# Products of k and v in a linear-attention kernel: one matmul a head on 128x64 tiles of TensorE in place of two on 128x32

## The chip, the cores and the metric

The kernel runs on one core of a Trainium2 chip. The metric is the device time of one execution in microseconds (us). TensorE (PE in the profile) multiplies, with its weight loads listed as an engine of their own (PEld); VectorE (DVE), ScalarE (ACT) and GpSimd (POOL) do elementwise work; SyncE (SP) issues transfers.

## The reference, cut to what matters

A recurrence with decay over 768 steps, for 4 batches and 8 heads of size 48, and behind it an MLP over the 3072 tokens (384 to 2048 to 384):

```python
for t in range(S):
    kt, vt, rt = (k[:, :, t], v[:, :, t], r[:, :, t])
    cur = np.einsum('bhd,bhe->bhde', u[None] * kt, vt)
    y[:, :, t] = np.einsum('bhd,bhde->bhe', rt, state + cur)
    state = w[None, :, :, None] * state + np.einsum('bhd,bhe->bhde', kt, vt)
...
h = x @ w_in
sp = np.maximum(h, 0.0) + np.log1p(np.exp(-np.abs(h)))
return (h * erf(sp)) @ w_out
```

The recurrence is computed in chunks of 128 steps. What a chunk adds to the state is, for each head, the product of its (scaled) k, transposed, with its v: a 48x48 matrix summed over 128 steps. The change is in how this product is cut into matmuls.

## The kernel before

There are 24 chunks, numbered g: six positions in the sequence, each for four batches. A chunk's tile `att` has k and v with the 128 steps on the partitions (columns K0 on: 8 heads of 48; columns V0 on: 4 pairs of 112, the two heads of a pair at 0 and 64). The work of a chunk on TensorE is, in words of the long string `ORDER`:

- `A`: the 128x128 products of r and k (`a_step`, line 328), written as tiles of 64 rows by 64 columns, with 48 rows of data (from chunk 8 on half of them with 128 moving columns and half with 64);
- `Y`: the output y (`y_product`, line 357) on tiles of 128 rows by 32 columns, from the state `sbd` and from the masked products `am`;
- `D`: the product of k and v (`ds_product`, line 380), for the chunks 0 to 19, since the last position needs no state behind it. Per head, two matmuls with 48 moving columns of v. The output of a head of 48 rows is cut into 32 rows and the rest (32 with 16 padding rows for the first head of a pair, 16 for the second), so that four matmuls of a pair of heads lie on the four column tiles of a 128x32 array;
- `X`, `V`, `T`: small products on full or on 64-column tiles (lines 414, 266, 271, 214, 217), in the first chunks only.

All operands here are float32, and the trace shows two records of MATMUL and two of LDWEIGHTS for each matmul of line 380: 20 chunks of 16 matmuls give 640 records. The MLP runs in 96 steps, each with `f` (line 436, 9 matmuls of 128x512) and `p` (line 499, 9 matmuls of 128x512), all on full 128x128 tiles.

`ORDER` is a hand-written order of all this work: each engine executes its part in this order, and waits where an operand or a buffer isn't ready. On TensorE a `D` stands mostly between the `Y` of its chunk and the `A` of a later one, or among `f` and `p`. Its result, in a PSUM buffer, is added to the state by VectorE (`s_wide`, line 394, for the first four chunks line 396), which the `Y` of the same batch one position later reads. The PSUM buffer is one of three that the `f` steps use as well.

Of the kernel before, what the change touches and what calls it, by code (L numbers as in the profile page):

```python
# [31 lines left out]
D = 48  # L32
NPAIR = 4
PR = 112
# [5 lines left out]
V0, K0, R0, AW = 1024, 1472, 1856, 2240  # L40
# [3 lines left out]
def body(ctx: ExitStack, tc: tile.TileContext, att, attn, wucol, u, win, wout, levels, outT):  # L44
    nc = tc.nc
# [106 lines left out]
    H = C // 2  # L152
# [222 lines left out]
    def ds_product(t, home, name):  # L375
        ds = home[0].tile([PR, NPAIR, D], F32, tag=home[1], name=name)
        for h in range(8):
            hh, p = h % 2, h // 2
            for c0, c1 in ((0, 32), (32, D if hh else H)):
                nc.tensor.matmul(out=ds[64 * hh + c0:64 * hh + c1, p, :], lhsT=t[:, K0 + h * D + c0:K0 + h * D + c1],  # L380
                                 rhs=t[:, V0 + PR * p + 64 * hh:V0 + PR * p + 64 * hh + D], start=True, stop=True,
                                 skip_group_check=True)
        return ds

    def s_views(b, hh):
# [180 lines left out]
    for i, x in enumerate(words):  # L566
# [44 lines left out]
        elif what == "M":  # L611
            st_[num // 10]["am", num % 10] = diag_m(st_[num // 10]["q"], num // 10, num % 10, eng, True)
        elif what == "A":
            st_.setdefault(num, {})
            a_step(num)
        elif what == "P":
            g, hh = num // 10, num % 10
            if g in direct:
                masked(g, hh)
            else:  # L620
                whole = slice(None)
                lo, hi = slice(0, H), slice(H, None)
                parts = [(whole, whole, hi), (lo, slice(0, 1), lo), (hi, slice(1, 2), lo)]
                predicated(st_[g]["am", hh], st_[g]["ap"][hh], parts if g >= LEAN else [(whole, whole, whole)])
        elif what == "Y":
            y_step(num)
        elif what == "X":
            x_step(num, sub)
        elif what == "D":
            st_.setdefault(num, {})["ds"] = ds_product(chunks[num], (ps3, "h"), f"ds{num}")  # L630
        elif what == "S":
            s_wide(num, sub, eng)
        elif what == "F":
            fetch_w(num // 10, num % 10)
        elif what == "C":
            load_w(sub, eng, num // 10, num % 10)
        elif what == "O":
            end(sub, num // 10, num % 10)
        elif what == "W":
            keep_warm(num)  # L640
# [12 lines left out]
    with tc.If(rv > 0), tc.tile_pool(name="gen", bufs=1) as gen:  # L653
# [37 lines left out]
        with tc.For_i(0, NB, 1) as blk:  # L691
            x = xp.tile([P, 2, NQ, TB], F32R, tag="x", name="gx")
            for b in range(4):
                t = apool.tile([P, AW], F32, tag="att", name=f"gatt{b}")
# [8 lines left out]
                for l in range(7):  # L703
# [7 lines left out]
                    for hh in range(2):  # L711
                        r = slice(64 * hh, 64 * hh + D)
                        ap = psa.tile([P, NPAIR, C], F32, tag="A", name=f"gA{b}_{l}_{hh}")
                        for p in range(NPAIR):
                            nc.tensor.matmul(out=ap[:, p, :], lhsT=kl[r, p].rearrange("p n m -> p (n m)"),
                                             rhs=rl[r, p].rearrange("p n m -> p (n m)"), start=True, stop=True)
# [3 lines left out]
                nc.vector.tensor_tensor(out=t[:, K0:R0], in0=t[:, K0:R0], in1=wknf, op=ALU.mult)  # L720
                y = y_product(t, am, b, False, f"gy{b}", False, (psa, "A"))
                ds = ds_product(t, (psa, "A"), f"gds{b}")
                for hh in range(2):
                    r, sv, w128 = s_views(b, hh)
# [155 lines left out]
```

## Time and profile before

| | us |
|---|---|
| median of 3 runs | 498.16 (497.91 to 498.21) |
| the profiled execution, its own time | 497.96 |
| its span, first to last instruction | 496.2 |
| TensorE busy (matmul) in the span | 487.1 (98%) |
| TensorE weight loads | 391.9 (79%) |
| ScalarE, VectorE, GpSimd busy | 388.9, 332.9, 148.5 |
| line 380 on the chain of waits | 1% of the span |

Busy times are unions of the records of a group, so records that overlap count once; the mean beside them is that of one record from its start to its modelled end. A matmul's record is much longer than its share of the array, since matmuls follow each other in a pipeline.

### The profile page before, as it was taken

What the parts mean: (1) busy time and instruction counts of PE and PEld (TensorE: products, weight loads), DVE (VectorE), ACT (ScalarE), POOL (GpSimd) and SP (SyncE); (2) the same over time, 40 slices, a digit from 0 to 9 for tenths busy, and PEclk for the clock granted to TensorE, in tenths of its full rate; (3) what the DMA queues carried; (4) which work ended last, traced back from release to release, by engine and by line L of the source; (5) the groups of instructions that cost most, each with busy time, mean ns of one, the idle gap of its engine ahead of it and who ended that gap; (6) DMA issues with size and microseconds to landing.
All of it is one profiled execution on the core that took longest, in us unless ns stands there. A gap on an engine that the chain in (4) does not pass through costs nothing.

```text
span 496.2 us, 10958 instructions
## 1 busy us (share of the span) xinstructions
PE 487.1 (98%) x4462; PEld 391.9 (79%) x4462; DVE 332.9 (67%) x586; ACT 388.9 (78%) x700; POOL 148.5 (30%) x132
## 2 busy tenths in 40 slices
PE   7999999999999999999999999999999999999995
PEld 5777888878778888888888878887878878888884
DVE  7999866767878956746766576686664445434553
ACT  2779999998976687877568875768977788978892
POOL 8659436016321735700168062172000000000000
PEclk9999999999999999999999999999999999999999
DMA  8874653328007603100450023232010000100001
GB/s 311 328 264 179 227 214 130 126 65 305 23 1 269 195 39 113 45 1 1 128 176 0 25 92 136 94 104 85 2 42 1 22 0 1 43 22 1 0 1 69
DMA packets 13864, 48.15 MB, mean 97 GB/s; under 512 B 1648, under 2 KB 2032, under 8 KB 13680
## 3 DMA queue, kind: packets, MB, share of 16 engines
q1 hardware_dynamic: 13808, 47.39, 27.2%
q8 instruction: 37, 0.61, 0.5%
q14 instruction: 19, 0.16, 0.1%
HBM read 41.09 MB, written 6.29 MB: 96 GB/s over the span
## 4 chain that ended last, share of the span: by engine, by line
PE 90%; DVE 5%; DMA 2%; issue 1%; SPq 1%; ACT 1%; POOL 0%; DVEq 0%; POOLq 0%
PE acc L499 40%; PE h L436 39%; PE y L357 6%; PE A L328 3%; DMA att<-in_att_dram 2%; PE ds L380 1%; DVE am L336 1%; DVE wt L139 1%; DVE gl L482 0%; DVE s L468 0%; DVE s L452 0%; SPq L71 0%; DVE q L297 0%; DVE att L249 0%; DVE wil L145 0%
## 5 line engine op out<-in xcount | busy, mean ns | idle before, releaser
L436 PE MATMUL h<-x,wih 128*128 128x512 f32 x576 | 182.8, 398 | 0.1
L436 PEld LDWEIGHTS h<-x,wih 128*128 128x128 f32 x576 | 107.2, 188 | 27.1 <-DVE s L468 0.8
L499 PE MATMUL acc<-gh,woh 128*128 128x512 f32 x288 | 115.2, 400 | 0.0
L499 PE MATMUL acc<-gl,woh 128*128 128x512 f32 x288 | 114.1, 396 | 0.3 <-DVE gl L482 0.3
L436 PE MATMUL h<-x,wil 128*128 128x512 f32 x288 | 113.9, 396 | 0.0
L499 PE MATMUL acc<-gh,wol 128*128 128x512 f32 x288 | 113.9, 395 | 0.0
L482 DVE TENSOR_TENSOR gl<-s,gh 128x512 fp32r<-128x512 f32 x96 | 70.0, 730 | 48.0 <-ACT gh L477 46.8
L468 DVE SCALAR_TENSOR_TENSOR s<-s,h 128x512 f32<-128x512 f32 x96 | 65.6, 685 | 49.0 <-ACT s L464 48.5
L452 DVE SCALAR_TENSOR_TENSOR s<-s,h 128x512 f32<-128x512 f32 x96 | 65.6, 686 | 37.7 <-ACT s L447 35.0
L456 ACT ACTIVATE s<-s 128x512 f32<-128x512 f32 x96 | 60.1, 627 | 25.4 <-DVE s L452 25.1
L443 ACT ACTIVATE s<-h 128x512 f32<-128x512 f32 x96 | 56.4, 590 | 26.1 <-PE h L436 25.7
L477 ACT CAST gh<-s 128x512 fp32r<-128x512 f32 x94 | 57.3, 612 | 19.4 <-DVE s L468 15.9
L499 PEld LDWEIGHTS acc<-gh,woh 128*128 128x128 f32 x288 | 54.2, 188 | 13.6 <-ACT s L456 0.2
L499 PEld LDWEIGHTS acc<-gl,woh 128*128 128x128 f32 x288 | 54.2, 188 | 13.2 <-DVE gl L482 0.7
L436 PEld LDWEIGHTS h<-x,wil 128*128 128x128 f32 x288 | 54.2, 188 | 13.0
L499 PEld LDWEIGHTS acc<-gh,wol 128*128 128x128 f32 x288 | 54.2, 188 | 12.9
L460 ACT ACTIVATE s<-s 128x512 f32<-128x512 f32 x96 | 60.4, 629 | 1.9
L447 ACT ACTIVATE s<-s 128x512 f32<-128x512 f32 x96 | 60.3, 629 | 1.7
L464 ACT ACTIVATE s<-s 128x512 f32<-128x512 f32 x96 | 60.0, 629 | 2.0
L553 POOL TENSOR_TENSOR att<-att,wrk 112x512 f32<-112x512 f32 x28 | 40.6, 1450 | 42.5 <-DMA att<-in_att_dram 36.9
L553 POOL TENSOR_TENSOR am<-idents,q 128x512 f32<-128x512 f32 x22 | 25.0, 1135 | 52.3 <-issue 24.0
L336 DVE COPY_PREDICATED am<-mask,A 64x128 f32<-64x128 uint32 (+2 forms) x108 | 38.0, 389 | 3.4 <-PE A L328 2.7
(89 smaller groups left out, 429.6 us busy)
## 6 DMA issues: line engine op xcount, KB each, us to landing
att<-in_att_dram SPq DMA_DIRECT2D x21, 608.0 KB, 6.0
att<-in_att_dram SPq DMA_DIRECT2D x23, 512.0 KB, 4.3
raw<-in_wout_dram SPq DMA_DIRECT2D x8, 768.0 KB, 5.5
raw<-in_win_dram SPq DMA_DIRECT2D x7, 768.0 KB, 4.4
out_dram<-o SPq DMA_DIRECT2D x18, 256.0 KB, 2.3
part<-o SPq DMA_DIRECT2D x6, 256.0 KB, 3.0
o<-part SPq DMA_DIRECT2D x6, 256.0 KB, 3.3
att<-in_att_dram SPq DMA_DIRECT2D x1, 1120.0 KB, 5.1
```

The source lines that it names most:

```text
L436: nc.tensor.matmul(out=h, lhsT=w[:, f, q, :], rhs=x[:, xi, q, :], start=k == 0, stop=k == 8)
L443: nc.scalar.activation(out=s1, in_=e["h"], func=AF.Tanh, bias=FB0, scale=FA0 * SHIFT)
L447: nc.scalar.activation(out=s1, in_=s1, func=AF.Tanh, bias=FB1, scale=FA1)
L452: nc.vector.scalar_tensor_tensor(out=e["s"], in0=e["s1"], scalar=FG / SHIFT, in1=e["h"], op0=ALU.mult, op1=ALU.add)
L456: nc.scalar.activation(out=s, in_=s, func=AF.Tanh, bias=FB2, scale=FA2 * SHIFT)
L460: nc.scalar.activation(out=s, in_=s, func=AF.Square, bias=FB3, scale=FA3)
L464: nc.scalar.activation(out=s, in_=s, func=AF.Square, bias=FB4, scale=FA4)
L468: nc.vector.scalar_tensor_tensor(out=s, in0=s, scalar=FC, in1=ff[n]["h"], op0=ALU.subtract, op1=ALU.mult, reverse0=True)
L477: nc.scalar.copy(out=e["gh"], in_=e["s"])
L482: eng.tensor_tensor(out=e["gl"], in0=e["s"], in1=e["gh"].bitcast(F32), op=ALU.subtract)
L499: nc.tensor.matmul(out=acc[e], lhsT=w[:, f, es], rhs=g, start=first and i == 0, stop=last and i == 2)
L553: i = nc.gpsimd.tensor_tensor(**kw)
```

## The change

For each head the two matmuls of line 380, on columns 0 to 31 and 32 on of its k, become one, on all of them: 64 columns for the first head of a pair (48 of its own and 16 of the next head's, which fall on padding rows, as the 16 did before), 48 for the second. The outputs are the same. The two heads of a pair lie on the two column tiles of a 128x64 array. A chunk has 8 such matmuls in place of 16. Nothing else is touched, and the order of the work is the same.

```diff
         for h in range(8):
             hh, p = h % 2, h // 2
-            for c0, c1 in ((0, 32), (32, D if hh else H)):
-                nc.tensor.matmul(out=ds[64 * hh + c0:64 * hh + c1, p, :], lhsT=t[:, K0 + h * D + c0:K0 + h * D + c1],
-                                 rhs=t[:, V0 + PR * p + 64 * hh:V0 + PR * p + 64 * hh + D], start=True, stop=True,
-                                 skip_group_check=True)
+            c1 = D if hh else H
+            nc.tensor.matmul(out=ds[64 * hh:64 * hh + c1, p, :], lhsT=t[:, K0 + h * D:K0 + h * D + c1],
+                             rhs=t[:, V0 + PR * p + 64 * hh:V0 + PR * p + 64 * hh + D], start=True, stop=True,
+                             skip_group_check=True)
```

## Rows read from the trace of the kernel before

**Rows 1.** Busy time by engine in three stretches (us; count of instructions in brackets).
```profile
0.00:57.00 57.00, 53.14 (x984) 41.04 (x985) 53.75 (x106) 40.74 (x80) 40.94 (x46) 1.00 0.74 271
57.00:331.00 274.00, 274.00 (x2516) 222.35 (x2515) 193.30 (x338) 219.36 (x389) 100.07 (x82) 1.00 0.31 105
331.00:496.20 165.20, 159.98 (x966) 128.46 (x964) 85.81 (x143) 128.77 (x233) 7.50 (x6) 0.99 0.06 23
```
**Rows 2.** The chain that ended last, by engine (the page's part 4).
```profile
PE 90%; DVE 5%; DMA 2%; issue 1%; SPq 1%; ACT 1%; POOL 0%; DVEq 0%; POOLq 0%
```
**Rows 3.** TensorE's groups by form: busy us, mean ns of one | idle before.
```profile
L328 PE MATMUL A<-att 48*64 48x128 f32 x448 | 17.1, 279 | 0.0
L380 PE MATMUL ds<-att 128*32 128x48 f32 x480 | 10.5, 207 | 0.0
L380 PE MATMUL ds<-att 128*16 128x48 f32 x160 | 10.0, 207 | 0.0
L328 PE MATMUL A<-att 48*64 48x64 f32 x256 | 6.6, 218 | 0.0
L266 PE MATMUL kt<-uw,att 112*128 112x2 f32 x16 | 2.1, 254 | 0.2 <-POOL att L553 0.2
```
**Rows 4.** Order of time on PE, 241.2 to 242.3 (start us, length us, what).
```profile
240.99 0.62 PE L357 MATMUL y<-am,att 128*32 128x128 f32 x16
241.43 0.86 PE L380 MATMUL ds<-att 128*32 128x48 f32 x64
242.22 0.34 PE L328 MATMUL A<-att 48*64 48x128 f32 x4
```
**Rows 5.** Records of line 380 in flight on PE, in four short stretches (count in brackets).
```profile
253.19:253.22 0.04, 0.03 (x4) 1.00 0.00 0
253.22:253.24 0.01, 0.01 (x4) 1.00 0.00 0
253.24:253.26 0.03, 0.03 (x8) 1.00 0.00 0
253.26:253.28 0.01, 0.01 (x8) 1.00 0.00 0
```
**Rows 6.** Order of time on PE and PEld around one D, 252.5 to 254.9.
```profile
252.32 1.06 PE L357 MATMUL y<-am,att 128*32 128x128 f32 x32
253.20 0.52 PE L380 MATMUL ds<-att 128*32 128x48 f32 x32
253.65 0.90 PE L328 MATMUL A<-att 48*64 48x128 f32 x32
253.09 0.49 PEld L380 LDWEIGHTS ds<-att 128*32 128x32 f32 x32
```
**Rows 7.** The same around the second D, 14.6 to 16.9.
```profile
15.15 0.60 PE L217 MATMUL tp<-idents,wrk 112*64 112x112 f32 x8
15.69 0.54 PE L380 MATMUL ds<-att 128*32 128x48 f32 x32
16.05 0.82 PE L357 MATMUL y<-am,att 128*32 128x128 f32 x19
15.69 0.41 PEld L380 LDWEIGHTS ds<-att 128*32 128x32 f32 x32
```
**Rows 8.** Line 217: durations in ns (min/median/max) of its loads and matmuls.
```profile
L217 PEld LDWEIGHTS tp<-idents,wrk x8: 132/136/138, 15.2 to 15.4; 112*64 112x64 f32 x8
L217 PE MATMUL tp<-idents,wrk x8: 259/259/310, 15.2 to 15.5; 112*64 112x112 f32 x8
```
**Rows 9.** Order of time on PE around a D between other shapes, 109.0 to 110.6.
```profile
108.85 0.90 PE L328 MATMUL A<-att 48*64 48x128 f32 x32
109.67 0.54 PE L380 MATMUL ds<-att 128*32 128x48 f32 x32
```
**Rows 10.** Waits of PE over the whole run: us in total, times, longest.
```profile
PE y L357 <- issue: 0.3, 1, 0.3
PE acc L499 <- DVE gl L482: 0.3, 1, 0.3
PE kt L266 <- POOL att L553: 0.2, 1, 0.2
PE y L357 <- DVE am L336: 0.2, 1, 0.2
```
**Rows 11.** Wait of PEld before the f step at 51.8.
```profile
PEld h L436 <- DVE sbd L394: 0.3, 1, 0.3
```

## The prediction

> **What bounds the kernel now.** I read first the busy time by engine in three stretches [rows 1]. From 57 to 331 us TensorE is busy for all of the 274 us, at full clock, while no other engine passes 220. What is added to or taken from TensorE there should move the end one for one. Before 57 us VectorE is the fuller engine (53.75 of 57 us), and TensorE has holes. The chain that ended last says the same: 90% PE [rows 2]. The last of the 20 D groups lies at 326 us, so none lies in the third stretch, which is only shifted.
>
> Then I read what a D costs. Its groups by form [rows 3] stand with 10.5 and 10.0 us, but these are unions that overlap, and a record's mean of 207 ns is its way through the pipeline. The distance that counts is the one at which records follow each other. Two D stand back to back in [rows 4]: 64 records take 0.86 us, one D alone 0.52 [rows 6], so 32 further records cost 0.34 us, 10.6 ns each. The short stretches show the pattern [rows 5]: four records are in flight, none is added for some 15 ns, then four more. So a **round** of four records, one on each column tile, takes 4 x 10.6 = 42.5 ns, and a D is 8 rounds: 0.206 (last record) + 7 x 0.0425 + some 0.02 (inside a round) = 0.52 us, as the row has it.
>
> **What sets the round.** Two candidates: the 48 moving columns, or the weight load. Form tells them apart. Line 328 has 64x64 tiles, four at once, loads of 64 columns, and in half its records 64 moving columns: 256 records in 16 chunks, busy 6.6 us [rows 3], so 0.4125 us for 4 rounds; less the last record's 0.218 and 0.02 inside the round, three rounds take 0.1745, or **58 ns** a round. Line 266 has only 2 moving columns behind loads of 128: 16 records in two groups of 8, 2.1 us, so (1.05 - 0.254)/7 = 114 ns a load. Twice 58 is 116, and the moving columns hardly matter there. So a load of 64 columns holds its tile for about 57 to 58 ns, and by the same scale one of 32 columns for some 29. Today's 42.5 ns is above 29: the round is set by the moving columns, the loads of 32 columns hide behind them.
>
> **The change part by part.** (1) *Half the matmuls.* They ran four at a time; now two run at a time. Each tile has 8 records before and after: on four tiles 2 for each of 4 pairs of heads, on two tiles the same 2. If 42.5 ns stays, a D takes as long as today. So the halved count is worth 0.
>
> (2) *Loads of 64 columns.* The first head's tile now loads 64 columns for each 48 moving ones. At 58 ns the load is longer than 42.5 and sets the round. 7 rounds cost 7 x (58 - 42.5) = 0.108 us more. The second head's tile loads 48 columns, some 43 ns, and is not late. I take 0.02 inside the round off, since there are only two tiles, and add the first load, below. Nothing hides this: TensorE is the engine that is full.
>
> (3) *A change of tiling more.* Today Y and D both use 128x32. Between them nothing drains: in [rows 6] the loads of D start at 253.09, the matmuls at 253.20, which is 0.18 us before the modelled end of Y at 253.38. Where the shape changes, it is otherwise. D to A in [rows 6]: D ends at 253.72, A starts at 253.65, 0.07 before. 64-column tiles to D, the very pair of shapes in question, in [rows 7]: the end is 15.75, the loads and matmuls start together at 15.69, 0.06 before. A to D in [rows 9]: 109.75 and 109.67, 0.08. So a change of shape costs **0.11 us** of overlap. After the change, Y to D is such a change, and where Y follows D, D to Y as well (today it starts 0.18 before D's end [rows 7]).
>
> (4) *The first load behind such a change lies open.* For 32 columns it is worth 0.02: a D takes 0.54 us behind another shape and 0.52 behind Y [rows 6, 7]. For 64 columns the first record of line 217 takes 310 ns against 259 [rows 8], 0.05. So a new D takes 0.206 + 7 x 0.058 + 0.02 to 0.05 = 0.63 to 0.66 us; I take 0.64, as part of the first load overlaps the next one.
>
> The 20 D are of four kinds, by what stands on either side on TensorE:
> - Y before it, another shape behind it (14, as [rows 6]): 0.64 - 0.52 = 0.12, and 0.11 for the change of shape: 0.23 each.
> - Another shape before it, Y behind it (3, as [rows 7]): 0.64 - 0.54 = 0.10, then 0.11 and 0.02 at the start of Y: 0.23 each.
> - Other shapes on both sides (2, as [rows 9]): 0.10 each.
> - Directly behind another D (1, [rows 4]): 8 rounds of 15.5 ns more, 0.12.
>
> From 55 us on there are 14 D: 10 of the first kind that follow at once (2.30), one of the first that starts late by a wait today already (0.10), one each of the others (0.23, 0.10, 0.12): 2.85 us, which TensorE can't hide.
>
> Before 55 us there are 6 D: three of the first kind, two of the second, one of the third, 1.25 us. Here there are waits that take some of it: 0.2 us for POOL right behind the first D, 0.2 and 0.3 in the next Y, 0.3 before line 499's first use of gl [rows 10], 0.3 before the f step at 51.8 [rows 11], of which about half is the drain that stays. Of the 1.25 the waits can take all that stands ahead of them, but the third to the fifth D (0.23 + 0.23 + 0.10) face only the 0.3 of gl, and the sixth (0.23) only about 0.15. I leave 0.3 us, between 0 and 1.25.
>
> **Sum:** 2.85 + 0.3 = 3.15 us. The profiled execution took 497.96 us, of which 496.2 are the span; it becomes 501.1. It lies 0.2 below the median of the runs, so against the median, 498.16 + 3.15 = **501.3 us**, 0.63% slower. VectorE gets the sum for the state some 0.1 to 0.2 us later; it is read one position later, so I cost that at nothing, and where VectorE is full (before 55 us) it would show as part of the 1.25.
>
> **The rivals.** *Drains alone.* A load of 64 columns hides behind 48 moving ones after all, because line 328's 58 ns are set by its 64 moving columns (64/48 x 42.5 = 57, which fits as well). Against it stands line 266. Then 14 late D cost 0.11 + 0.02 for 10, 0.13 for one and next to nothing for the others: 1.4 us, 499.6.
>
> *Loads alone.* A switch between 128x64 and 128x32 drains nothing. [Rows 7] speak against it. 20 D at some 0.1: 1.4 to 2 us, 499.9.
>
> *Loads of the two tiles one after the other.* A round would take 53 + 40 ns of load and some 5 more, 98 ns, and a D 0.27 us longer than I forecast: 14 late ones add 3.8, some 505. Against it: four loads of 64 columns share a 58 ns round in line 328, though with 48 rows each and not 128. The Trainium skill, TensorE: Matmul & The Clock Gate, section Part 3: Packing small matmuls, says that a weight load overlaps matmuls in flight only when its row group differs, and all tiles here have the same rows; by that rule the time would go this way. The round of 42.5 ns in [rows 4], shorter than a 32-column load and 48 moving columns one after the other, speaks against the rule for today's tiles.
>
> *Faster: the number of records sets the pace.* If the queue that feeds TensorE takes some 10.6 ns a record, and four in flight is chance, then 16 records fewer save 16 x 10.6 = 0.17 us a D, and the change of shape gives back 0.11. For the 10 full D that is -0.06 each, for the others -0.05 to -0.17; with the early ones absorbed some -1.2 us, 497.0. It turns in favour once a round of two tiles is shorter than about 28 ns. The bursts of four in [rows 5] speak against it: records enter within a round far faster than 10.6 ns apart. The Trainium skill, TensorEngine Tiling (Array Packing), section Instruction Overhead, gives each matmul about 60 cycles; for 320 records at 2.4 GHz that would be an estimated 8 us saved, and the 10.6 ns per record of this trace are below such an overhead.
>
> **How the numbers follow.** My forecast (load and drain, 500.4 to 502.5, by the 0 to 1.25 of the early D and 0.63 to 0.66 of the length) gets 0.74; drains alone 0.08, loads alone 0.05, loads one after the other 0.06, faster 0.04, and 0.03 that all is taken up somewhere (same). A measurement can tell about 0.2%, 1 us, from no change, so 499.16 is the border to slower; of drains alone a third falls below it. Slower 0.90, same 0.06, faster 0.04. The range takes in the two cases near 499.6 and stretches above my forecast's upper end, since the early D could cost more than their share: 499.3 to 503.0.
>
> **What would show it.** In the profile of the changed kernel, line 380 has 320 records of 128x64 and 128x48; a D is 0.64 us long (0.52 if the load hides, 0.9 if loads take turns, under 0.4 if records set the pace). D starts 0.07 before the end of Y, not 0.18. TensorE stays full from 57 to 331 us, and the f and p steps are as long as before. The prediction is wrong if D keeps 0.52, if its loads run ahead under Y, or if the delays vanish in waits of TensorE before 55 us and after.

## The result

The changed kernel takes **501.40 us** at the median (500.92 to 504.32), the kernel before 498.16 (497.88 to 498.73): a ratio of 1.0074 (of the means; two of the seven runs took 503.13 and 504.32), 95% interval 1.0054 to 1.0095. By the medians it is slower by 3.2 us; the forecast was 501.3, 3.15 us more.

Busy time by engine in three stretches of the changed kernel (columns as in [rows 1]):

```profile
0.00:57.00 57.00, 53.30 (x871) 41.59 (x872) 53.72 (x106) 40.88 (x81) 41.77 (x46) 1.00 0.74 267
57.00:331.00 274.00, 274.00 (x2295) 220.81 (x2294) 192.70 (x331) 217.65 (x386) 99.33 (x81) 1.00 0.31 102
331.00:499.70 168.70, 163.17 (x979) 130.88 (x977) 88.98 (x151) 130.46 (x236) 7.80 (x6) 0.99 0.08 29
```

TensorE is busy all through the middle stretch, as before [rows 1], and it gets through less work in it: 2295 records in place of 2516. Of the 221 fewer, 208 are the thirteen D of this stretch, halved, and 13 have moved into the third stretch (979 in place of 966). The granted clock is the same in all three. So the time is lost inside TensorE's work, not in a wait for another engine.

Line 380 by form in the changed kernel (busy us, mean ns of one):

```profile
L380 PE MATMUL ds<-att 128*64 128x48 f32 x160 | 13.1, 226 | 0.0
L380 PE MATMUL ds<-att 128*48 128x48 f32 x160 | 11.0, 213 | 0.0
```

The 160 records with loads of 64 columns cover 13.1 us; in [rows 3] the 480 with loads of 32 covered 10.5. Order of time around the same D that [rows 6] show (start us, length us):

```profile
254.79 0.51 PE L357 MATMUL y<-am,att 128*32 128x128 f32 x12
255.23 0.67 PE L380 MATMUL ds<-att 128*64 128x48 f32 x16
255.83 0.34 PE L328 MATMUL A<-att 48*64 48x128 f32 x4
...
255.23 0.54 PEld L380 LDWEIGHTS ds<-att 128*64 128x64 f32 x16 [0.20 <-issue]
```

Both predicted terms can be read here. D starts at 255.23, 0.07 before the modelled end of Y at 255.30; in [rows 6] it started 0.18 before it, with its loads 0.29 before. Now loads and matmuls start together, and the load engine sat idle for 0.20 us before them, waiting for nothing that the profile shows. And D takes 0.67 us where it took 0.52.

The starts of D's 16 records, one by one, in ns from the first, with the columns of the load:

```
64 columns:   0   93  151  210  268  326  385  443
48 columns:   6   86  131  176  221  266  311  356
```

The two tiles run side by side, at their own pace. The moving columns are 48 on both; the pace is 58.3 ns with loads of 64 columns and 45 with loads of 48, behind a longer first step. D is as long as the slower tile.

The delay against the kernel before adds up along the same work: the `f` step behind the sixth D starts at 51.79 (51.82 before), the D at 109.67 in [rows 9] at 109.86, that at 253.20 in [rows 6] at 255.23, and the last matmul at 493.84:

```profile
493.84 0.39 PE L499 MATMUL acc<-gh,wol 128*128 128x512 f32 x1
```

In the kernel before it is

```profile
490.63 0.40 PE L499 MATMUL acc<-gh,wol 128*128 128x512 f32 x1
```

So TensorE is 3.21 us later at its end; the other 0.3 of the two profiles' spans (499.7 and 496.2) lies behind the last matmul, in the way of the output.

### The profile page after: what moved, and what is told of

It reads as the page before. It is cut to its first block, busy times and chain, and to the rows that moved or that the text cites. A ratio compares the mean times of both kernels' runs of the same rounds, so it can differ in the third digit from the quotient of the medians.

```text
span 499.7 us, 10319 instructions
## 1 busy us (share of the span) xinstructions
PE 490.5 (98%) x4142; PEld 393.3 (79%) x4142; DVE 335.4 (67%) x586; ACT 389.0 (78%) x700; POOL 148.9 (30%) x132
## 4 chain that ended last, share of the span: by engine, by line
PE 93%; DMA 3%; DVE 1%; ACT 1%; SPq 0%; issue 0%; DVEq 0%
PE h L436 40%; PE acc L499 39%; PE y L357 7%; PE A L328 3%; PE ds L380 2%; DMA raw<-in_win_dram 2%; DMA att<-in_att_dram 1%; DVE am L336 1%; DVE s L452 0%; ACT s L456 0%; ACT am L308 0%; SPq L71 0%; PE y L414 0%; DVE s L468 0%; DVE gl L482 0%
## 5 line engine op out<-in xcount | busy, mean ns | idle before, releaser
L482 DVE TENSOR_TENSOR gl<-s,gh 128x512 fp32r<-128x512 f32 x96 | 71.5, 746 | 48.1 <-ACT gh L477 46.8
```

What stands on the lines that cost most here:

```text
L482: eng.tensor_tensor(out=e["gl"], in0=e["s"], in1=e["gh"].bitcast(F32), op=ALU.subtract)
```

## The experiments

**Where the D stand.** Two kernels give the new form to some D alone:

```diff
+        wide = name[2:].isdigit() and int(name[2:]) in (0, 1, 2, 3, 4, 6)     # early
+        wide = name[2:].isdigit() and int(name[2:]) not in (0, 1, 2, 3, 4, 6) # late
...
-            for c0, c1 in ((0, 32), (32, D if hh else H)):
+            end = D if hh else H
+            for c0, c1 in ((0, end),) if wide else ((0, 32), (32, end)):
```

> Only the six D before 57 us (chunks 0 to 4 and 6) get the new form, the other fourteen keep the old one. Theory A (TensorE's waits on VectorE and GpSimd before 57 us take up all that these six D cost): 498.2 us, within 0.3 of the kernel before, though each of the six D is 0.44 us from its first to its last start where it was 0.32 or 0.34. Theory B (my recorded share): 498.5 us. Theory C (each D costs its price wherever it stands, 1.25 us in all): 499.4 us.

> Only the fourteen D from 55 us on get the new form. Theory A: all of the loss is here, 3.2 us, so 501.4 us, as the changed kernel. Theory B: 501.1 us. Theory C: 500.2 to 500.4 us, with the rest in the early D.

The early kernel took 497.86 us, ratio 0.9997 (0.9988 to 1.0006); the late one 501.23, ratio 1.0065 (1.0051 to 1.0078). The late fourteen cost all that the change costs (3.27 us by the medians), and the early six nothing that can be measured. The times alone don't rule out the 0.3 us on record, which is the upper end of the early kernel's interval; the traces speak for theory A. The last of the early D stands in the early kernel so:

```profile
50.06 0.40 PE L357 MATMUL y<-am,att 128*32 128x128 f32 x8
50.39 0.67 PE L382 MATMUL ds<-att 128*64 128x48 f32 x16
50.99 1.10 PE L328 MATMUL A<-att 48*64 48x128 f32 x32
52.02 0.50 PE L438 MATMUL h<-x,wih 128*128 128x512 f32 x1
```

Each D has its full price there too (0.67 us). The `f` step behind it is 0.2 us late (52.02 against 51.82). The late kernel, with the old D up to there, starts this step at 51.98, and the changed kernel, with the new D, at 51.79, so this much is scatter between executions. In the early kernel it is gone later: the last matmul starts at 490.54, before the 490.63 of the kernel before. What takes it up are waits of the weight loads for VectorE between 120 and 135 us, 0.6 us in the kernel before and 0.2 in the early one.

**The change of shape by itself.** Seven heads in the old form, then one (64 columns) in the new one, so that each D has one change from 128x32 to 128x64 more:

```diff
-        for h in range(8):
+        for h in (0, 1, 2, 3, 4, 5, 7, 6):
...
-            for c0, c1 in ((0, 32), (32, D if hh else H)):
+            end = D if hh else H
+            for c0, c1 in ((0, end),) if h == 6 else ((0, 32), (32, end)):
```

> The old form for seven heads, and the new form for one (head 6, 64 columns), put last: in each D one change from 128x32 to 128x64 is added and no second one, since the shape changes behind D anyway in most places. If a change of shape drains the array: the first seven heads take 0.32 us from first to last start (two tiles still have 8 records), then 0.13 until the 64-column load, 0.08 between its two records and 0.15 to the next shape, 0.68 where it was 0.45, so 0.23 a D and 3.2 us for the fourteen late D: 501.4 us. If nothing drains between the two shapes, the two records ride along: at most 0.05 a D, 498.2 to 498.9 us.

It took 501.91 us, ratio 1.0085 (1.0062 to 1.0108), the forecast's 501.4 within its interval. Order of time around one D:

```profile
285.30 0.84 PE L357 MATMUL y<-am,att 128*32 128x128 f32 x24
285.96 0.77 PE L381 MATMUL ds<-att 128*32 128x48 f32 x30
286.66 0.45 PE L328 MATMUL A<-att 48*64 48x128 f32 x8
```

D starts 0.18 before the end of Y, so there is no drain between equal shapes, and it is 0.77 us long. Record by record, the 28 old ones start within 0.317 us as before, the first of 64 columns 0.136 after the last of them, which is 0.07 before that one's modelled end (206 ns), the second 0.093 later. What these two wait for isn't their own half of the array: head 6 lies on columns 0 to 63, whose last old record started some 0.1 us before that of head 7 on columns 64 to 127. So from 128x32 to 128x64 the whole array drains. The rival in which only the loads cost would have had the two records ride along.

**The width of the load by itself.** The first head of a pair loads 48 columns, from chunk 4 on. Its 16 padding rows are then not written, so VectorE has to leave them out. The control has VectorE's two instructions with loads of 64:

```diff
+        late_d = name[2:].isdigit() and int(name[2:]) >= 4      # not in the control
...
-            c1 = D if hh else H
+            c1 = D if hh or late_d else H      # not in the control
...
-            nc.vector.tensor_tensor(out=sv, in0=sv, in1=ds, op=ALU.add)
+            for r in (slice(0, D), slice(H, PR)):
+                nc.vector.tensor_tensor(out=sv[r], in0=sv[r], in1=ds[r], op=ALU.add)
```

> The new form, but from chunk 4 on the first head of a pair loads 48 columns too, as the second does. The 16 padding rows between the heads are then not written, so VectorE adds the two heads' rows with two instructions in place of one; the results are the same. If the 64-column load sets the pace: both tiles go at 45 ns a record, D is 0.35 us from first to last start in place of 0.44, and the next shape follows after 0.135 in place of 0.151: 0.11 less a D, 1.5 us in all, 499.9 us. If the load width doesn't matter (the change of shape and the two tiles alone cost): D stays at 0.44 and the time at 501.4 us.

It took 504.33 us, ratio 1.0128 (1.0112 to 1.0143): D did what was forecast, the time did not.

> The control for the kernel with loads of 48 columns: the new form with its loads of 64 columns, and VectorE's sum for the state split in two instructions as there. If the split on VectorE is what made that kernel slower than forecast: D is 0.44 us here where it was 0.36 there, 0.10 less a D with the way to the next shape, so this kernel is 1.4 to 1.5 us slower than that one: 505.8 us. If the width of the load is worth nothing in time: both take the same, 504.3 us.

> The kernel with loads of 48 columns from chunk 4 on again, beside its control: 504.3 us, D 0.357 us from its first to its last start.

The control took 505.85 us, ratio 1.0161 (1.0144 to 1.0178), and the kernel with loads of 48 beside it 504.50, ratio 1.0136 (1.0119 to 1.0153): 1.35 us between the medians, where 1.4 to 1.5 was expected. The two intervals overlap at their edges, so the times by themselves are weak evidence for this; D is clear. One D of the kernel with loads of 48, and one of the control:

```profile
287.83 0.51 PE L357 MATMUL y<-am,att 128*32 128x128 f32 x12
288.28 0.56 PE L381 MATMUL ds<-att 128*48 128x48 f32 x16
288.77 0.67 PE L328 MATMUL A<-att 48*64 48x128 f32 x16
```

```profile
289.23 0.67 PE L380 MATMUL ds<-att 128*64 128x48 f32 x16
```

The first is 0.56 us long against 0.67, and both its tiles go at 45 ns a record; record by record, the next shape follows 0.495 us after the start of every late D against 0.595 in the control. The width of the load is what makes D long. What my first expectation left out was VectorE, which has two instructions in place of one in the sum for the state. Part of the price shows as waits of TensorE that the changed kernel doesn't have, the `f` step waiting for a PSUM buffer that VectorE still reads:

```profile
PE h L438 <- DVE sbd L396: 1.7, 3, 0.6
```

So without that detour the form with 48 columns would save an estimated 1.4 us of the changed kernel's time (14 late D at 0.10), and would still be slower than the kernel before: 0.56 us for a D in place of 0.52, and the change of shape.

**Which of load and moving columns sets the pace.** The moving columns are widened to 64, in the old form and in the new one:

```diff
-        ds = home[0].tile([PR, NPAIR, D], F32, tag=home[1], name=name)
+        wide = home[0].tile([PR, NPAIR, H], F32, tag=home[1], name=name)
+        ds = wide[:, :, 0:D]
...
-                                 rhs=t[:, V0 + PR * p + 64 * hh:V0 + PR * p + 64 * hh + D], start=True, stop=True,
+                                 rhs=t[:, V0 + PR * p + 64 * hh:V0 + PR * p + 64 * hh + H], start=True, stop=True,
```

> The old form with 64 moving columns of v for each head in place of 48; the 16 further output columns are never read. If the moving columns set the old round: 56 ns in place of 42.5, D 0.41 us from first to last start in place of 0.32, 1.3 us more, 499.5 us. If the loads or the number of records set it: no change, 498.2 us.

> The new form with 64 moving columns in place of 48, the further output columns never read. If the 64-column load sets the pace of the first head's tile at 58 ns: 64 moving columns take 56 and hide behind it, D stays at 0.44 us and the time at 501.4 us; only the second head's tile goes from 45 to 56 ns a record. If moving columns set the new pace too: 13.5 ns more for each of 7 steps, 1.3 us in all, 502.7 us.

The old form took 499.40 us, ratio 1.0026 (1.0015 to 1.0036), the new one 501.00, ratio 1.0058 (1.0042 to 1.0075). One D of each, the old form first:

```profile
284.89 0.63 PE L381 MATMUL ds<-att 128*32 128x64 f32 x32
```

```profile
285.81 0.68 PE L381 MATMUL ds<-att 128*64 128x64 f32 x16
```

A third more moving columns lengthen the old D from 0.52 to 0.63, with rounds of 56 ns, and leave the new one at 0.68 (0.67). The first was bound by its moving columns, the second by its loads.

**Twice the loads for the same moving columns.** Each matmul is cut into two of 24 moving columns:

```diff
-            nc.tensor.matmul(out=ds[64 * hh:64 * hh + c1, p, :], ...
+            for e in (0, D // 2):
+                v0 = V0 + PR * p + 64 * hh + e
+                nc.tensor.matmul(out=ds[64 * hh:64 * hh + c1, p, e:e + D // 2], ..., rhs=t[:, v0:v0 + D // 2], ...
```

> The new form with each matmul cut into two of 24 moving columns: twice the 64-column loads, the same moving columns in all. If the load sets the pace: 16 records at 58 ns on the first head's tile, D 0.91 us from first to last start in place of 0.44, 6.5 us more than the changed kernel, 507.9 us. If the moving columns set it: no change, 501.4 us.

> The old form with each matmul cut into two of 24 moving columns: twice the loads of 32 columns. If the round is the longer of load and moving columns, the load of 32 now sets it, at some 31 ns (26.7 by the scale of the 64-column load, and 4.5): 16 rounds, 0.49 us in place of 0.32, 2.4 us more than before, 500.6 us. If the old round of 42.5 ns was already the load's: 16 rounds of it, 0.66 us, 502.9 us. If only the moving columns counted: 498.2 us.

The new form took 510.83 us, ratio 1.0270 (1.0247 to 1.0293):

```profile
154.94 1.11 PE L382 MATMUL ds<-att 128*64 128x24 f32 x32
```

Its records start over 0.896 us, by the load's pace (0.91 expected). The time is 2.9 us above the expectation at the median and 1.9 in the profiled execution (509.77). Most of this has a plain cause: I had added up the fourteen late D alone, and here the early six cost too much for the waits before 57 us; the D that starts at 55.74 in the changed kernel starts at 57.99.

The old form took 509.34 us, ratio 1.0226 (1.0206 to 1.0246), against an expectation of 500.6, a miss:

```profile
293.00 0.78 PE L382 MATMUL ds<-att 128*32 128x24 f32 x64
```

Within D a tile's records follow each other at 31.6 ns in bursts, the pace expected of a 32-column load. But after the first two dozen or so the four tiles no longer run in step, each pauses in turn, and the 64 records need 0.594 us and not 0.49, 9.4 ns a record. A D behind Y costs 0.26 us more than the old one and not 0.17, which is 3.4 us for the late fourteen. The rest of the 11.2 us (509.34 against 498.13) is of another kind. Before 57 us the kernel loses 6.2 us, and TensorE stands still for 4.0 of them in three stalls of up to 2.5 us; behind 57 us there are two more, 1.3 us together. The stalls lie in D and in A, and TensorE waits in them for nothing that the profile shows:

```profile
PE A L328 <- issue: 2.9, 2, 2.5
...
PE ds L382 <- issue: 2.3, 3, 1.1
```

After the longest of them the granted clock falls to half, 1.2 GHz, so part of the 6.2 us is run at that level. The A in which TensorE stood still, and a stretch behind it with its granted clock, 0.50:

```profile
22.88 0.57 PE L328 MATMUL A<-att 48*64 48x128 f32 x11 [2.50 <-issue]
...
24.30:27.60 3.30, 3.30 (x53) 3.03 (x57) 3.30 (x7) 2.27 (x4) 0.00 (x0) 0.50 0.04 14
```

To see whether the number of records has a floor near there, half the moving columns of the old form were left out, with as many records as before (VectorE's sums are halved too, which the lines leave out):

```diff
-        ds = home[0].tile([PR, NPAIR, D], F32, tag=home[1], name=name)
+        ds = home[0].tile([PR, NPAIR, D // 2], F32, tag=home[1], name=name)
...
-                                 rhs=t[:, V0 + PR * p + 64 * hh:V0 + PR * p + 64 * hh + D], start=True, stop=True,
+                                 rhs=t[:, V0 + PR * p + 64 * hh:V0 + PR * p + 64 * hh + D // 2], start=True, stop=True,
```

> The old form with only the first 24 of the 48 columns of v in each product (the other half of the state is left out, and VectorE's sums are half as long): as many records as before, half the moving columns. What is read is D alone. If a round is the longer of the 32-column load (31.6 ns in the bursts of the cut kernel) and the moving columns: 7 x 31.6 + 20 = 0.24 us from first to last start. If TensorE is fed a record only every 9.4 ns or so, as the whole of the cut D suggests (64 records in 0.595): 31 x 9.4 = 0.29 us. If the number of records had set the old pace, 0.32 as before.

Two D of it, the first behind a Y and the second behind another shape (498.33 us in one run, of which only D is read):

```profile
284.07 0.46 PE L380 MATMUL ds<-att 128*32 128x24 f32 x32
```

```profile
109.46 0.45 PE L380 MATMUL ds<-att 128*32 128x24 f32 x32
```

Their records start over 0.275 and 0.256 us. Both are below the old form's 0.317, so the number of records did not set the old pace. In the second D, whose loads could not run ahead, the load is the whole: each tile with loads of 32 columns goes at 31.6 ns to its end, 7 x 31.6 = 221 ns, and 21 for the first load, which lies open, and 14 inside the round make 256. In the first, 24 records follow at the same pace, 0.168 us, and the last 8 take 0.107 us, 13 ns each. In the D of the cut kernel above it is 28 records in 0.225 us and then 36 in 0.369, 10.2 ns each. So it isn't a fixed price for every record, but something that sets in behind the first two dozen records or so. What it is, is left open.

## Why the prediction was right

**The bound.** That the late D would move the end one for one held: 3.21 us at the last matmul, all from D behind 55 us (the late kernel), and TensorE was full throughout.

**Part 1, the halved count worth nothing.** Held. The rival in which the number of records sets the pace was nearer than I had put it: where moving columns were narrow, the later records of a D came 10 to 13 ns apart, and the old pace was 10.2 (0.317 us over 31 steps). It was still wrong for the old form: as many records took 0.411 us with 64 moving columns and 0.256 to 0.275 with 24.

**Part 2, the load of 64 columns.** Held in mechanism and size: 58.3 ns measured, 58 predicted from line 328 [rows 3]. The doubt noted under the rivals, that line 328's pace could come from its 64 moving columns, is settled by the kernel with loads of 48 beside its control, by the cut kernel and by the two tiles of one D at 58 and 45 ns. The scale was a little off for narrower loads: 31.6 ns for 32 columns where I had 29, and 45 for 48 where I had 43, so the second head's tile is also slower than 42.5, which the slower tile beside it hides.

**Part 3, the change of shape.** Held: 0.07 before the end of Y in place of 0.18. One step of the sorting was wrong. I counted the second D [rows 7] among those with another shape before them; but what stands before it is line 217 on 64-column tiles, the very shape that D now has. There a change of shape goes away:

```profile
15.15 0.60 PE L217 MATMUL tp<-idents,wrk 112*64 112x112 f32 x8
15.59 0.62 PE L380 MATMUL ds<-att 128*48 128x48 f32 x16
```

D starts 0.16 before the end of line 217 at 15.75, in [rows 7] 0.06. It stands before 55 us, so it moved nothing.

**Part 4 and the kinds.** The length of D was 0.67 us and not 0.64. The first load behind the change of shape lies open with 0.035 (93 ns to the second record, then 58), within the 0.02 to 0.05 that I had given. A term was missing: the last record, with a load of 64 columns, lasts 222 ns and not 206, and behind it the next shape starts 0.016 later. 7 x 0.0583 + 0.035 + 0.222 = 0.665. By the delay of the next matmul that isn't D's, the kinds cost 0.255 (predicted 0.23), 0.258 at the late one of the second kind (0.23), 0.124 (0.10) and 0.381 for the two D in a row (0.35). The fourteen late D sum to 3.15 us, 2.85 predicted; waits for VectorE near 125 us add 0.1 in this profile.

**The early D.** Mis-sized the other way: 0.3 us taken, nothing measured. In the changed kernel the waits before 52 us have taken up all 1.25 (the `f` step at 51.79 against 51.82). The two errors cancel. That the sum fits to 0.1 us is luck; its parts fit to 0.3.

**VectorE at nothing.** Held. Its waits for D grew from 5.2 us to

```profile
DVE sbd L394: 7.8, 10
```

and moved nothing. The experiment with the split sum shows what that cover is worth: where VectorE has one instruction more for a D, TensorE waits.

**The rivals.** Drains alone and loads alone each have their half: the two kernels that isolate them show both. Loads one after the other are excluded, since the tiles' trains of 58 and 45 ns run side by side on the same 128 rows; taking turns would have made a round of 103 ns.

## What to carry to other kernels

For small float32 matmuls on column tiles, compare two paces per tile before merging them: that of the moving columns and that of the weight load, which grew with its columns in all these runs. Fewer and wider matmuls gained nothing while the moving columns set the pace, and lost once the load was longer. And look at the shapes of the neighbours: here a matmul group in the same tile shape as the one before it started 0.18 us before that one's end; in another shape it started 0.07 before it, when the array had drained, and then showed its first load.

## What the runs showed of the hardware beyond that

- A tile's pace by its moving columns was 42.5 ns for 48 and 56 for 64; by its load 31.6 ns for 32 columns (in bursts), 45 for 48, 58.3 for 64, each the longer of the two where both were there. The load was hidden behind the tile's own running matmuls; it was not added to them.
- Four tiles with 16 records each and 24 moving columns went at the load's pace for the first two dozen records or so and then fell out of step, 9.4 ns a record over the whole D. With 8 records each it was 8.9 behind a Y, and 8.3, all of it the load's pace, behind another shape. In the former kernel TensorE also stood still for up to 2.5 us with nothing in the profile to wait for, and after that stall its granted clock was 0.50 for a stretch. The cause of the pauses and of the stalls wasn't found.
